# Two attentions mixed by a gate: output products summed in one block, denominators inverted in a narrow tile, a cubic for part of the exponentials

## The chip, the cores and the metric

The kernel runs on one core of a Trainium2 chip. The metric is the device time of one execution in microseconds, the median of three runs. A core has five instruction queues that run beside each other: TensorE (PE in the profile, its weight loads PEld), VectorE (DVE), ScalarE (ACT), GpSimd (POOL) and SyncE (SP), which here only issues DMAs. Each queue runs its instructions in the order in which they stand; between queues there are semaphores.

## The reference

Two attentions with 32 heads of 16 over the same 2048 rows of `x` (512 columns), mixed row by row by a gate. In A all heads share one key and one value head; B is full multi-head attention.

```
g = sigmoid((x * gate_w).sum(-1))
# A: q = x@wq (32 heads of 16), k = x@wk, v = x@wv (one head of 16)
# B: q, k, v = x@wqkv (32 heads of 16 each)
p = softmax(q @ k.T * 16**-0.5)          # 2048 x 2048 for each head
a = (p @ v, heads side by side) @ wo     # likewise b
out = g * a + (1 - g) * b
```

## The kernel before

**Tiling.** The heads are taken in eight groups of eight, A and B in turn (`groups`: a0, b0, a1, b1, ... b3). A group is done in four phases: two halves of the 2048 queries, and in each half two sets of head pairs (`q` is 0 or 2). So there are 32 phases. A phase goes over the keys in 32 *quads*, and a quad consists of two *units*: one unit is a score tile of 128 x 1024, eight matmuls on TensorE (`products`, L627). That makes 2048 units, and each needs its exponential. ScalarE takes most of them (L641, out of PSUM into a `prob` tile). VectorE takes some, two units at a time, by exponent and mantissa bits and four Horner steps (`chain`, L843 to L856, seven instructions a unit). The values of a quad are then multiplied and summed over the phase in one PSUM bank (L682). V carries a column of ones, so the softmax denominators come out of the same product.

**Banks.** Two score tiles `sc` alternate between TensorE and ScalarE. Two other banks, `pair[0]` and `pair[1]` (they print as pair_82 and pair_83, and swap roles now and then), hold the running sum over values and everything else: projections of q, k and v, scores for VectorE, and output products. The second role is called *spare* below; one job at a time owns the spare bank until VectorE has emptied it.

**End of a phase.** VectorE copies the full bank to `raw` (L747). SP moves its rows apart into numerators `oT` and denominators `dT`, both 128 x 512 and with each denominator repeated 16 times, once for each row of its head (`normalised`, L565). VectorE inverts `dT` in two pieces (L572), multiplies (L575) and splits the result into two f16 parts `o16` (L578, L581).

**Output products.** When both phases of a half of a group are normalised, four *output units* (`o_unit`) follow, one for each pair of 128-query tiles. A unit is six products with `wo` in the spare bank (two phases, three hi/lo combinations). VectorE multiplies by the gate while it empties the bank, in two instructions of 128 x 512 (L521), into one of two `sum` tiles, and a DMA of POOL adds the tile to `out` in DRAM (L531). For the last group the sum so far is read back into `late` (L1136) and added on VectorE (L515). The last phase of all is normalised and multiplied in four pieces of 128 columns after the loop (L572 to L581 and L1295); its output units hold only the first phase of that half.

**What sets the order.** The program is written out by a planner that runs when the kernel is built. It holds a clock for each engine and a cost for each kind of instruction, and asks again and again what TensorE or VectorE does next (`pe_step`, `_Plan.vector`). On TensorE scores come first as soon as a score tile is free by the plan; other work goes between two scores only if it ends before the next. When the plan allows it, `vector_job` gives two units to VectorE. The loop over phases ends when no unit and no VectorE operation is left, and only then the pieces of the tail are written.

Of the kernel before, what the change touches and what calls it, by code (L numbers as in the profile page):

```python
# [12 lines left out]
F32 = mybir.dt.float32  # L13
# [7 lines left out]
P = 128  # L21
# [14 lines left out]
S_MAX = 40.0  # L36


VEC = (0.14718679, 0.3602188, 0.76941108, -0.03925424)
LEAD = struct.unpack("I", struct.pack("f", 3.46474126))[0] & 0x7FFFFF  # L40
# [10 lines left out]
PROBS, VECS = 6, 6  # L51
# [116 lines left out]
def _fast(ctx, tc, x, wq_a, wk_a, wv_a, wo_a, wqkv_b, wo_b, gate_w, out, flag):  # L168
# [23 lines left out]
    sums = [big.tile([P, 2, BLK], F32, name=f"sum{n}") for n in range(2)]  # L192
# [82 lines left out]
    x_tiles = (vec_tiles + sums)[:8]  # L275
# [145 lines left out]

    def project(part, src, gi, half, kind, can, due):
# [17 lines left out]
        def finish(t):  # L440
# [9 lines left out]
            def then(end):  # L450
                free["spare"] = end + FROM_VEC
                plan.vec(lambda: absmax(kind, 2 * gi + half, hilo[0], AX.XY), 1130, 4, end, due=end + 8000)
                if part == "v":
                    turned(gi, half, hilo, end)
                else:
                    put(hilo, end)
# [6 lines left out]
                     lambda now: ready.get(need, math.inf) <= now and free["hilo"] <= now and can(), due, name, lambda now: can())  # L463

    def turned(gi, half, hilo, now):
# [26 lines left out]
        units.append(_Unit(jobs, finish, lambda now: True, lambda: 0, f"turn{gi}{half}"))  # L492
# [3 lines left out]
    def o_unit(n, half, t, qs, first, last):  # L496

        src, gi = groups[n]
        w, i = weights[src, gi, "o"], "ab".index(src)
        steps = [(q, a, b) for q in qs for a, b in PARTS]  # L500
        tt = [8 * half + t, 8 * half + 4 + t]
        mine = late[:, 4 * half + t]
        state = {}

        def job(k):
            q, a, b = steps[k]
            lhs = [o16s[n, half, q][:, a, t * P : (t + 1) * P]] * 2
            rhs = [w[e ^ (q // 2)][:, b] for e in range(2)]
            by_tiles(pair[1], lhs, rhs, k == 0, k == len(steps) - 1)

        def finish(end):
            def take(e):
                g = gate_up[:, i, tt[e] : tt[e] + 1]
                if n + 1 == len(groups):
                    nc.vector.scalar_tensor_tensor(mine[:, e], pair[1][:, e], g, mine[:, e], op0=ALU.mult, op1=ALU.add)  # L515
                    if last:
                        (nc.sync, nc.scalar)[e].dma_start(out[tt[e] * P : (tt[e] + 1) * P, :], mine[:, e])
                    return
                if e == 0:
                    state["sum"] = sums[state["turn"]]  # L520
                nc.vector.tensor_scalar(state["sum"][:, e], pair[1][:, e], g, None, op0=ALU.mult)  # L521

            def then(t):
                free["spare"] = t + FROM_VEC
                if n + 1 == len(groups):
                    return
                dst = out.rearrange("(h e t p) d -> h t p e d", h=2, e=2, p=P)[half, t_]
                if n == 0:
                    done = plan.on_sp([lambda: nc.sync.dma_start(dst, state["sum"])], t, ISSUE_SP)
                else:  # L530
                    done = plan.on_pool([lambda: nc.gpsimd.dma_start(dst, state["sum"], accum_op=ALU.add)], t, 1300)  # L531
                sum_free[state["turn"]] = done + SUM_LANDS

            t_ = t
            begin = end + TO_VEC
            if n + 1 < len(groups):
                state["turn"] = turn[0]
                turn[0] ^= 1
                begin = max(begin, sum_free[state["turn"]])
            for e in range(2):  # L540
                plan.vec(lambda e=e: take(e), 660, 1, begin, (), then if e else None)
# [3 lines left out]
        due = 32 * (4 * n + 2 * half + 8)  # L545
        return _Unit(jobs, finish, lambda now: all(made(("o16", n, half, q), math.inf) <= now for q in qs)
                     and made(("wo", src, gi), math.inf) <= now and made("gates", math.inf) <= now
                     and (sum_free[turn[0]] <= now + 4000 if n + 1 < len(groups) else made("late", math.inf) <= now), lambda: starts_in(due), f"o{n}{half}{t}")

    turn, sum_free = [0], [0.0, 0.0]  # L550

    def normalised(n, half, q, raw, now):
# [10 lines left out]
        moves = [(*move, e) for t in (d, o) for e in range(2) for move in moves if move[0] is t]  # L563
        for m, (part, at, to, n_rows, e) in enumerate(moves):
            queues[m % len(queues)].dma_start(part[ROWS * e + to :][:n_rows], raw[at, e])  # L565
        plan.sp = max(plan.sp, now) + len(moves) * ISSUE_SP
        o16 = ops.tile([P, 2, BLK], F16, tag="o16", name=f"o16{n}{half}{q}", bufs=7)
# [5 lines left out]

        def times(c):
            nc.vector.scalar_tensor_tensor(o[:, c : c + cut], o[:, c : c + cut], UP, d[:, c : c + cut], op0=ALU.mult, op1=ALU.mult)  # L575
# [10 lines left out]
        due = now + 30000  # L586

# [3 lines left out]
        for c in range(0, BLK, cut):  # L591
            a = plan.vec(lambda c=c: over(c), 1560, 3.5, now + 7700, (), None, due)
            b = plan.vec(lambda c=c: times(c), 330, 3.4, now + 12000, (a,), None, due)
            e = plan.vec(lambda c=c: high(c), 200, 3.3, 0.0, (b,), None, due)
            plan.vec(lambda c=c: low(c), 330, 3.2, 0.0, (e,), then if c else None, due)
# [134 lines left out]
    def emptied(t):  # L730
        ph = pv_at[0]
        n, half, q = phases[ph]
# [735 lines left out]
```

## Time and profile before

| | |
|---|---|
| median of three runs | 1826.78 us (1826.64 to 1827.12) |
| profiled execution, first to last instruction | 1822.2 us |
| what lies around the span (median less span) | 4.6 us |
| ScalarE busy | 1778.7 us, 98% |
| TensorE busy | 1742.1 us, 96% |
| VectorE busy | 1332.0 us, 73% |

The profiled execution has no total of its own beside its span; the runs agree within 0.03%, so the 4.6 us between the span and their median stand for launch and end. TensorE's matmuls are pipelined and their ends are modelled, so its 96% is not a measure of how full it is.

### The profile page before, as it was taken

What the parts mean: (1) busy time and instruction counts of PE and PEld (TensorE: products, weight loads), DVE (VectorE), ACT (ScalarE), POOL (GpSimd) and SP (SyncE); (2) the same over time, 40 slices, a digit from 0 to 9 for tenths busy, and PEclk for the clock granted to TensorE, in tenths of its full rate; (3) what the DMA queues carried; (4) which work ended last, traced back from release to release, by engine and by line L of the source; (5) the groups of instructions that cost most, each with busy time, mean ns of one, the idle gap of its engine ahead of it and who ended that gap; (6) DMA issues with size and microseconds to landing.
All of it is one profiled execution on the core that took longest, in us unless ns stands there. A gap on an engine that the chain in (4) does not pass through costs nothing.

```text
span 1822.2 us, 95700 instructions
## 1 busy us (share of the span) xinstructions
PE 1742.1 (96%) x44697; PEld 844.5 (46%) x44697; DVE 1332.0 (73%) x1507; ACT 1778.7 (98%) x1942; POOL 305.1 (17%) x367
## 2 busy tenths in 40 slices
PE   8999999999999999999999999999999999999896
PEld 5544444444444444444444444444444444444442
DVE  5277656779667597869767569796967676788994
ACT  5999999999999999999999999999999999999995
POOL 2212001202020131231102023133200111012000
PEclk9999999999999999999999999999999999999998
DMA  5121111323121142433212123342312122236111
GB/s 152 36 61 44 46 58 55 90 55 67 32 62 32 39 83 55 75 65 66 44 42 63 32 66 56 67 84 63 64 20 57 44 55 57 42 67 149 36 61 61
DMA packets 64883, 109.39 MB, mean 60 GB/s; under 512 B 14480, under 2 KB 22928, under 8 KB 64480
## 3 DMA queue, kind: packets, MB, share of 16 engines
q0 software_dynamic: 21504, 43.99, 13.6%
q1 hardware_dynamic: 39744, 56.99, 11.4%
q8 instruction: 351, 5.75, 1.3%
q10 hardware_dynamic: 3232, 2.23, 0.4%
q14 instruction: 52, 0.43, 0.1%
HBM read 14.75 MB, written 33.55 MB: 27 GB/s over the span
## 4 chain that ended last, share of the span: by engine, by line
ACT 86%; issue 8%; PE 4%; DVE 1%; DMA 1%; ACTq 0%; POOL 0%; DVEq 0%
ACT prob L641 85%; PE pair L682 1%; PE sc L627 1%; PE pair L301 0%; DVE vec L856 0%; PE pair L1173 0%; DMA prob<-in_A_wv_dram 0%; DVE xT L1295 0%; DMA vec<-in_A_x_dram 0%; DVE xT L515 0%; DMA Qa<-loqa 0%; PE pair L335 0%; DVE dT L572 0%; ACT early L641 0%; PE pair L210 0%
## 5 line engine op out<-in xcount | busy, mean ns | idle before, releaser
L641 ACT ACTIVATE prob<-sc 128x1024 f32<-128x1024 f32 x1905 | 1749.7, 1134 | 3.8 <-PE sc L627 3.2
L682 PE MATMUL pair<-prob,vA 64*32 64x512 f32 (+1 forms) x8048 | 510.4, 566 | 0.0
L682 PE MATMUL pair<-prob,vB 64*32 64x512 f32 (+1 forms) x8016 | 508.4, 569 | 0.0
L856 DVE SCALAR_TENSOR_TENSOR vec<-vec,vec 128x1024 f32<-128x1024 f32 x366 | 445.9, 1242 | 2.8
L627 PE MATMUL sc<-Qb,K 64*32 64x512 f16 x7632 | 395.9, 380 | 37.2 <-ACT prob L641 26.8
L627 PE MATMUL sc<-Qa,kA 64*32 64x512 f16 x7776 | 401.8, 380 | 21.7 <-ACT prob L641 11.6
L627 PEld LDWEIGHTS <-K 64*32 64x32 f16 x8192 | 201.2, 89 | 414.8 <-issue 375.1
L627 PEld LDWEIGHTS <-kA 64*32 64x32 f16 x8192 | 199.8, 89 | 390.2 <-issue 346.6
L843 DVE TENSOR_SCALAR vec<-pair 128x1024 int32<-128x1024 f32 x122 | 148.4, 1216 | 64.5 <-PE pair L627 64.4
L682 PEld LDWEIGHTS pair<-prob,vA 64*32 64x32 f32 x8048 | 155.3, 105 | 20.0 <-issue 1.4
L682 PEld LDWEIGHTS pair<-prob,vB 64*32 64x32 f32 x8016 | 153.5, 105 | 19.0 <-DVE raw L747 0.7
L856 DVE SCALAR_TENSOR_TENSOR vec<-vec 128x1024 f32<-128x1024 f32 x122 | 151.8, 1247 | 0.6
L531 POOL DMA_DIRECT2D out_dram<-sum x48 | 60.6, 1284 | 387.6 <-DVE sum L521 373.0
L572 DVE RECIPROCAL dT<-dT 128x256 f32<-128x256 f32 (+1 forms) x66 | 111.4, 1694 | 18.9 <-DMA dT<-raw 18.6
L747 DVE COPY raw<-pair 128x1024 f32<-128x1024 f32 x31 | 37.9, 1224 | 95.8 <-PE pair L682 95.2
L847 DVE TENSOR_SCALAR vec<-vec 128x1024 int32<-128x1024 int32 x122 | 84.1, 692 | 2.8 <-PE pair L682 1.3
L851 DVE TENSOR_SCALAR vec<-vec 128x1024 int32<-128x1024 int32 x122 | 84.5, 695 | 0.0
L521 DVE TENSOR_SCALAR sum<-pair,gate_up 128x512 f32<-128x512 f32 x112 | 78.6, 740 | 6.3 <-PE pair L210 6.0
L404 POOL DMA_DIRECT2D Qa<-hiqa x31 | 17.3, 558 | 305.6 <-DVE hiqa L445 284.5
L210 PEld LDWEIGHTS <-o 64*32 64x32 f16 x3072 | 50.1, 93 | 39.3 <-ACT o L578 8.1
L404 POOL DMA_DIRECT2D Qb<-hiqb x32 | 18.4, 574 | 293.3 <-DVE o L578 169.1
L210 PE MATMUL pair<-w16ob,o 64*32 64x512 f16 x1488 | 61.1, 384 | 6.0 <-ACT o L578 6.0
(160 smaller groups left out, 1182.7 us busy)
## 6 DMA issues: line engine op xcount, KB each, us to landing
out_dram<-sum POOLq DMA_DIRECT2D x48, 512.0 KB, 5.8
vB<-vB SPq DMA_DIRECT2D x16, 384.0 KB, 4.9
dT<-raw SPq DMA_DIRECT2D x32, 128.0 KB, 3.1
oT<-raw SPq DMA_DIRECT2D x32, 128.0 KB, 3.4
out_dram<-sum SPq DMA_DIRECT2D x8, 512.0 KB, 2.9
xT<-out_dram SPq DMA_DIRECT2D x16, 256.0 KB, 3.3
dT<-raw SPq DMA_DIRECT2D x62, 64.0 KB, 2.2
out_dram<-xT SPq DMA_DIRECT2D x12, 256.0 KB, 2.4
```

The lines of the kernel that those rows point to most:

```text
L210: nc.tensor.matmul(outs[n : n + COLS, i], lhs[i][rows(i), n : n + COLS], rhs[i][rows(i)], start=start, stop=stop)
L521: nc.vector.tensor_scalar(state["sum"][:, e], pair[1][:, e], g, None, op0=ALU.mult)
L531: done = plan.on_pool([lambda: nc.gpsimd.dma_start(dst, state["sum"], accum_op=ALU.add)], t, 1300)
L572: nc.vector.reciprocal(d[:, c : c + cut], d[:, c : c + cut])
L627: nc.tensor.matmul(bank[a : a + COLS, hh], k[rows(hh), key : key + COLS], Q[src, gi, half, p][rows(hh), j * BLK : (j + 1) * BLK], start=Tr ...
L641: nc.scalar.activation(probs[u], sc, AF.Exp, scale=SCALE / (UP * UP))
L682: nc.tensor.matmul(pair[0][32 * k : 32 * k + 32, i, cols], v[rows(i)], probs[2 * m + k // 2][rows(i), hh, cols], start=first, stop=last)
L747: nc.vector.tensor_copy(state["raw"], full)
L843: nc.vector.tensor_scalar(tile("p").bitcast(I32), pair[1], SCALE / (UP * UP) / math.log(2) * 2.0 ** 23, None, op0=ALU.mult)
L847: nc.vector.tensor_scalar(tiles["m"].bitcast(I32), tiles["p"].bitcast(I32), 0x7FFFFF, 125 << 23, op0=ALU.bitwise_and, op1=ALU.bitwise_or)
L851: nc.vector.tensor_scalar(tiles["w"].bitcast(I32), tiles["p"].bitcast(I32), 0x7F800000, 0x40000000 | LEAD, op0=ALU.bitwise_and, op1=ALU.bi ...
L856: nc.vector.scalar_tensor_tensor(p, m if i == 3 else p, VEC[i], m if i else w, op0=ALU.add, op1=ALU.mult)
```

## The change

Four things change, and since the planner knows all of them, the order of everything between the first and the last score moves with them.

**1. One block of output products for A and B.** The gate moves from the emptying of the spare bank into the normalisation. A unit is now built for a pair of groups (a and b of the same index): twelve products, from four normalised blocks, in one accumulation; the last half has nine, since the last phase is left to the tail. VectorE empties the bank in one instruction of 128 x 1024 with a constant. One `sum` tile is left instead of two; the place of the other as an input tile is taken by a piece of `vB[1]`.

**2. Denominators in a narrow tile.** The denominators of a phase, eight rows of 512, go from `raw` to DRAM (`held`), come back as 128 x 32 (`each`), are inverted there and multiplied with the gate (`gate_in`, which is laid out once through DRAM), go to DRAM again (`back`) and come back with each row read 16 times into `dT`. The tail keeps the old way.

**3. A cubic for B on VectorE.** For units of B the chain has three instructions (`first`, `second`, `third`). The limit on B's scores in the final range check gets tighter (`B_MAX`), and for that q of B is measured by head, as sums over the head on TensorE (`magnitudes`).

**4. Later moves.** q and k are laid out (`behind`, `reads`) only when the plan has passed the last reader of their buffers.

```diff
+CUBE = (0.5500864384102879, 0.8808852829622843, -0.986763876, 1.22848465)
+PROBS, VECS, SUMS = 6, 6, 1
...
     def o_unit(j, half, t, done, last):
+        steps = [(n, q, a, b) for n, q in done for a, b in PARTS]
...
+            def take():
+                if ends:
+                    nc.vector.scalar_tensor_tensor(mine, pair[1], UP ** -2, mine, op0=ALU.mult, op1=ALU.add)
...
+                nc.vector.tensor_scalar(state["sum"], pair[1], UP ** -2, None, op0=ALU.mult)
...
     def normalised(n, half, q, raw, now):
+            each = ops.tile([P, 2 * DH], F32, tag="each", name=f"each{n}{half}{q}", bufs=1)
...
+                nc.sync.dma_start(held.rearrange("(e h) q -> h e q", e=2)[to : to + count], raw[which])
+            nc.sync.dma_start(each, held.rearrange("h (c j) -> (h c) j", c=DH))
...
+        def gated():
+            nc.vector.reciprocal(each, each)
+            nc.vector.scalar_tensor_tensor(each, each, UP, gate_in[:, "ab".index(src), half], op0=ALU.mult, op1=ALU.mult)
...
+                nc.sync.dma_start(back.rearrange("h (c j) -> (h c) j", c=DH), each)
+                for e in range(2):
+                    for h in range(4):
+                        nc.sync.dma_start(d[ROWS * e + h * DH :][:DH], back[4 * e + at : 4 * e + at + 1].to_broadcast([DH, BLK]))
...
     def emptied(t):
+            parts = [(m, r) for m, r in ((n - 1, 0), (n - 1, 2), (n, 0), (n, 2))]
+            if src == "b" and (n + 1 < len(groups) or half == 0):
                 if q:
+                    units.extend(o_unit(n // 2, half, t, parts, True) for t in range(4))
+            elif src == "b" and q == 0:
+                units.extend(o_unit(n // 2, half, t, parts[:3], False) for t in range(4))
...
     def chain(u, t):
+            def first():
+                nc.vector.tensor_scalar(tile("p"), pair[1], CUBE[0] * SCALE / (UP * UP), CUBE[1], op0=ALU.mult, op1=ALU.add)
+            def second():
+                nc.vector.scalar_tensor_tensor(tile("w"), tiles["p"], CUBE[2], tiles["p"], op0=ALU.add, op1=ALU.mult)
+            def third():
+                nc.vector.scalar_tensor_tensor(p, w, CUBE[3], p, op0=ALU.add, op1=ALU.mult)
```

**How the order moves.** Counted over the whole program, ScalarE's exponentials go from 1926 to 1920 and VectorE's units from 122 to 128, of which 38 belong to A and 90 to B. Three places follow.

The first is VectorE's queue in the last group, two units of B: before, with the seven steps of one unit woven into others (`vec` are VectorE's own tiles, `pair` the spare bank).

```order
L843 TENSOR_SCALAR vec_108<-pair_83 128x1024
L847 TENSOR_SCALAR vec_106<-vec_108 128x1024
L843 TENSOR_SCALAR vec_104<-pair_83 128x1024
L851 TENSOR_SCALAR vec_105<-vec_108 128x1024
L856 SCALAR_TENSOR_TENSOR vec_108<-vec_106 128x1024
L747 COPY raw_40921<-pair_82 128x1024
```

Now two whole units stand in six rows:

```order
L962 TENSOR_SCALAR vec_105<-pair_83 128x1024
L965 SCALAR_TENSOR_TENSOR vec_106<-vec_105 128x1024
L969 SCALAR_TENSOR_TENSOR vec_105<-vec_106,vec_105 128x1024
L962 TENSOR_SCALAR vec_108<-pair_83 128x1024
L965 SCALAR_TENSOR_TENSOR vec_107<-vec_108 128x1024
L969 SCALAR_TENSOR_TENSOR vec_108<-vec_107,vec_108 128x1024
```

Each step of the cubic reads what the step before it wrote, and nothing else stands between them.

The second is SP's queue at the end of two phases of A, before (`raw` is the copied bank, `dT` the denominators, `oT` the numerators, Qb a later q of B):

```order
L565 DMA dT_36036<-raw_36033 64x512 x2
L565 DMA oT_36035<-raw_36033 64x512 x2
L565 DMA dT_37304<-raw_37301 64x512 x2
L565 DMA oT_37303<-raw_37301 64x512 x2
L404 DMA Qb_37613<-hiqb_37573 32x1024
```

The same kind of place now; `held` and `back` lie in DRAM:

```order
L219 DMA vB_92<-vB_91 64x1536 x2
L615 DMA held_37151<-raw_37146 4x2x512
L617 DMA each_37150<-held_37151 128x32
L619 DMA oT_37148<-raw_37146 64x512 x2
L634 DMA back_37152<-each_37150 128x32
L638 DMA dT_37149<-back_37152 16x512 x8
```

Four DMAs of a phase of A have become thirteen, and three of the steps wait for a landing or for VectorE in front of them.

The third is VectorE's queue at the end of the program. Before, the last of the output units (L515, two rows each) stand ahead of the last copy of a phase (L744), and the tail begins right behind it:

```order
L581 TENSOR_TENSOR o_40935<-oT_40923,o_40935 128x256
L515 SCALAR_TENSOR_TENSOR xT<-pair_83,gate_up,xT 128x512 x8
L744 COPY raw_42005<-pair_82 128x512
L572 RECIPROCAL dT_42009<-dT_42009 128x128
L575 SCALAR_TENSOR_TENSOR oT_42008<-oT_42008,dT_42009 128x128
```

Now three output units are emptied between that copy and the tail's first reciprocal, out of the bank that the copy reads:

```order
L652 TENSOR_TENSOR o_40574<-oT_40560,o_40574 128x256 x2
L560 SCALAR_TENSOR_TENSOR xT<-pair_83,xT 128x1024 x3
L821 COPY raw_41823<-pair_82 128x512
L560 SCALAR_TENSOR_TENSOR xT<-pair_82,xT 128x1024 x3
L626 RECIPROCAL dT_41827<-dT_41827 128x128
L644 SCALAR_TENSOR_TENSOR oT_41826<-oT_41826,dT_41827 128x128
```

On TensorE their 27 products stand behind the last values of the last phase; before, none stood there.

## Rows read from the trace of the kernel before

**Rows 1.** Page, part 1: busy us, share of span, instructions, by engine.
```profile
PE 1742.1 (96%) x44697; PEld 844.5 (46%) x44697; DVE 1332.0 (73%) x1507; ACT 1778.7 (98%) x1942; POOL 305.1 (17%) x367
```

**Rows 2.** Groups by line, ScalarE's exponentials: xcount | busy us, mean ns | idle before.
```profile
L641 ACT ACTIVATE prob<-sc 128x1024 f32<-128x1024 f32 x1905 | 1749.7, 1134 | 3.8 <-PE sc L627 3.2 <-DVE xT L515 0.5
L641 ACT ACTIVATE vec<-sc 128x1024 f32<-128x1024 f32 x10 | 10.2, 1035 | 0.5 <-PE sc L627 0.5
L641 ACT ACTIVATE early<-sc 128x1024 f32<-128x1024 f32 x8 | 8.4, 1047 | 0.3 <-ACT prob L641 0.3
L641 ACT ACTIVATE vB<-sc 128x1024 f32<-128x1024 f32 x3 | 3.1, 1026 | 0.6 <-PE sc L627 0.6
```

**Rows 3.** Timeline of ScalarE, first and last exponentials: start, us, what, xcount.
```profile
28.11 5.66 ACT L641 ACTIVATE prob<-sc 128x1024 f32<-128x1024 f32 x6 [1.20 <-PE sc L627]
...
1769.46 31.38 ACT L641 ACTIVATE prob<-sc 128x1024 f32<-128x1024 f32 x34
```

**Rows 4.** Two stretches: window, us, then busy (xcount) PE PEld DVE ACT POOL.
```profile
300.00:500.00 200.00, 192.09 (x4920) 91.97 (x4911) 155.31 (x171) 199.84 (x219) 31.36 (x32) 1.00 0.26 62
1500.00:1700.00 200.00, 191.77 (x4880) 91.23 (x4865) 159.65 (x180) 199.43 (x219) 29.13 (x34) 1.00 0.38 78
```

**Rows 5.** Waits: who, for whom: us in total, times, longest.
```profile
PE sc L627 <- ACT prob L641: 38.4, 108, 0.5
ACT prob L641 <- PE sc L627: 3.2, 8, 1.2
DVE dT L572 <- DMA dT<-raw: 18.6, 6, 4.4
```

**Rows 6.** Groups by line, VectorE.
```profile
L843 DVE TENSOR_SCALAR vec<-pair 128x1024 int32<-128x1024 f32 x122 | 148.4, 1216 | 64.5 <-PE pair L627 64.4
L851 DVE TENSOR_SCALAR vec<-vec 128x1024 int32<-128x1024 int32 x122 | 84.5, 695 | 0.0
L856 DVE SCALAR_TENSOR_TENSOR vec<-vec,vec 128x1024 f32<-128x1024 f32 x366 | 445.9, 1242 | 2.8
L856 DVE SCALAR_TENSOR_TENSOR vec<-vec 128x1024 f32<-128x1024 f32 x122 | 151.8, 1247 | 0.6
L572 DVE RECIPROCAL dT<-dT 128x256 f32<-128x256 f32 x62 | 107.6, 1742 | 15.7 <-DMA dT<-raw 15.4
L521 DVE TENSOR_SCALAR sum<-pair,gate_up 128x512 f32<-128x512 f32 x112 | 78.6, 740 | 6.3 <-PE pair L210 6.0
L448 DVE SCALAR_TENSOR_TENSOR lovb<-pair,hivb 128x1024 f16<-128x1024 f32 x8 | 9.8, 1224 | 0.3
```

**Rows 7.** DMA issues: xcount, KB each, median us to landing.
```profile
out_dram<-sum POOLq DMA_DIRECT2D x48, 512.0 KB, 5.8
xT<-out_dram SPq DMA_DIRECT2D x16, 256.0 KB, 3.3
dT<-raw SPq DMA_DIRECT2D x62, 64.0 KB, 2.2
```

**Rows 8.** Timeline of SP, one phase of B: issue of four DMAs.
```profile
922.58 3.67 SPq L565 DMA_DIRECT2D dT<-raw  x4
```

**Rows 9.** Timeline of the program's end.
```profile
1796.67 0.41 PE L210 MATMUL pair<-w16ob,o 64*32 64x512 f16 x8
...
1800.12 0.63 PE L210 MATMUL pair<-w16ob,o 64*32 64x512 f16 x16
...
1800.83 1.41 DVE L515 SCALAR_TENSOR_TENSOR xT<-pair,gate_up,xT 128x512 f32<-128x512 f32 x2 [2.26 <-PE pair L210]
...
1802.87 0.59 ACT L745 COPY raw<-pair 128x512 f32<-128x512 f32 x1 [2.04 <-DVE raw L744]
...
1806.04 0.95 DVE L572 RECIPROCAL dT<-dT 128x128 f32<-128x128 f32 x1 [3.20 <-DMA dT<-raw]
```

**Rows 10.** Two stretches of the end; behind POOL stands TensorE's granted clock.
```profile
1802.00:1804.40 2.40, 0.00 (x0) 0.00 (x0) 0.84 (x2) 0.59 (x1) 0.64 (x1) 1.00 0.14 36
1804.50:1811.20 6.70, 3.24 (x64) 0.91 (x64) 4.87 (x10) 0.89 (x3) 0.99 (x2) 0.50 0.24 62
```

More of the change, by code (lines that the diff above doesn't have):

```diff
@@ L420, in starts_in, with behind, reads @@
         return plan.act + 2 * max(m - at[0], 0) * EXP * 0.93
+    waiting = []
+    def behind(m, fn):
+        waiting.append((m, fn))
+    def reads():
+        for m, fn in list(waiting):
+            if at[0] >= m and not (half_vec and half_vec[0] // 2 < m):
+                waiting.remove((m, fn))
+                fn(plan.pe)
     def project(part, src, gi, half, kind, can, due):
@@ L455, in then @@
                 else:
-                    put(hilo, end)
+                    s = 2 * (2 * gi + (src == "b")) + half
+                    behind(64 * (s - 1) if part == "q" else 256 * gi, lambda t: put(hilo, max(t, end)))
             free["hilo"] = math.inf
@@ L491, in turned, with o_unit @@
         jobs = [(lambda ts=ts: job(ts), HALF) for ts in (range(4), range(4, 8))]
-        units.append(_Unit(jobs, finish, lambda now: True, lambda: 0, f"turn{gi}{half}"))
+        units.append(_Unit(jobs, finish, lambda now: pv_at[0] >= 8 * gi, lambda: 0, f"turn{gi}{half}"))
     o16s = {}
[L496 to L500, printed above, removed]
+    def o_unit(j, half, t, done, last):
+        steps = [(n, q, a, b) for n, q in done for a, b in PARTS]
@@ L518, in take, with then @@
                     return
[L519 to L525, printed above, removed]
+                state["sum"] = sums[state["turn"]]
+                nc.vector.tensor_scalar(state["sum"], pair[1], UP ** -2, None, op0=ALU.mult)
+            def then(now):
+                free["spare"] = now + FROM_VEC
+                undone[j, half] -= 1
+                if ends:
@@ L535, in finish @@
+                if j == 0:
+                    at = plan.on_sp([lambda: nc.sync.dma_start(dst, state["sum"])], now, ISSUE_SP)
+                else:
+                    at = plan.on_pool([lambda: nc.gpsimd.dma_start(dst, state["sum"], accum_op=ALU.add)], now, 1300)
+                sum_free[state["turn"]] = at + SUM_LANDS
             begin = end + TO_VEC
-            if n + 1 < len(groups):
+            if not ends:
                 state["turn"] = turn[0]
-                turn[0] ^= 1
+                turn[0] = (turn[0] + 1) % SUMS
@@ L539, in finish @@
                 begin = max(begin, sum_free[state["turn"]])
-            for e in range(2):
-                plan.vec(lambda e=e: take(e), 660, 1, begin, (), then if e else None)
+            plan.vec(take, 1131, 1, begin, (), then)
         made = ready.get
         jobs = [(lambda k=k: job(k), PRODUCT) for k in range(len(steps))]
[L545 to L548, printed above, removed]
@@ L550, in _fast @@
-    turn, sum_free = [0], [0.0, 0.0]
+        due = 32 * (8 * j + 2 * half + 8)
+        undone[j, half] = undone.get((j, half), 0) + 1
+        return _Unit(jobs, finish, lambda now: all(made(("o16", n, half, q), math.inf) <= now and made(("wo", *groups[n]), math.inf) <= now for n, q in done)
+                     and (made("late", math.inf) <= now if ends else sum_free[turn[0]] <= now + 6000), lambda: starts_in(due), f"o{j}{half}{t}")
+    undone = {}
+    turn, sum_free = [0], [0.0] * SUMS
     def normalised(n, half, q, raw, now):
@@ L586, in normalised, with spreads @@
         due = now + 30000
+        begun = [math.inf]
         def then(end):
             ready["o16", n, half, q] = end + FROM_VEC
[L591 to L595, printed above, removed]
+        def spreads(end):
+            spread(end)
+            for c in range(0, BLK, cut):
+                b = plan.vec(lambda c=c: times(c), 330, 3.4, begun[0], (), None, due)
+                e = plan.vec(lambda c=c: high(c), 200, 3.3, 0.0, (b,), None, due)
+                plan.vec(lambda c=c: low(c), 330, 3.2, 0.0, (e,), then if c else None, due)
+        plan.vec(gated, 430, 3.5, now + 7500, (), spreads, due,
+                 room=lambda: ready.get("gates", math.inf) <= plan.dve)
     tail = []
```

138 lines of the change are left out of this document (104 added, 34 removed).

## The prediction

> **What bounds the kernel now.** I read the busy shares first: ScalarE 98%, TensorE 96%, VectorE 73% [rows 1]. TensorE's figure says little, so the second view is the groups by line. ScalarE's exponentials have four rows, 1905 + 10 + 8 + 3 = 1926 instructions [rows 2]. The third view is the timeline of ScalarE: the first exponential starts at 28.11, the last group of 34 ends at 1769.46 + 31.38 = 1800.84 [rows 3]. So the span of 1822.2 has a head of 28.1, 1772.7 with exponentials, and a tail of 21.4, in which ScalarE hardly works. From start to start an exponential takes (1772.7 - 1.1) / 1925 = 0.920 us on the whole. In the windows ScalarE makes 219 of them in 200 us, in the stretch from 300 as in that from 1500, which is 0.913 each [rows 4]. The difference, 0.007 x 1926 = 14 us, is lost here and there along the run. The waits say who leads: TensorE waited 108 times for ScalarE to free a score tile, 38.4 us, and ScalarE 8 times for scores, 3.2 us [rows 5]. So the middle of the program is as long as the number of ScalarE's exponentials makes it, and VectorE, with a quarter of its time free, sets nothing there.
>
> I work against the profiled span of 1822.2 and add the 4.6 us that separate it from the median of 1826.78; the profiled execution shows no other total.
>
> **The change part by part.**
>
> *Exponentials.* A unit on VectorE costs 1.216 + 2 x 0.695 (L847 is like L851) + 3 x 1.242 + 1.247 = 7.58 us before. The cubic has the reading from PSUM, one step with one tile and one with two: 1.216 + 1.247 + 1.242 = 3.71 us [rows 6]. With 38 units of A and 90 of B that is 38 x 7.58 + 90 x 3.71 = 622 us where 122 x 7.58 = 925 us stood. VectorE gains 303 us, but the order gives it only six units more. Six exponentials less on ScalarE are 6 x 0.913 = **5.5 us less**. They count in full as long as TensorE keeps the pace; it gets no fewer score products, the same number of output products, and 32 matmuls more for the magnitudes.
>
> *Inversions and emptying.* 62 x 1.742 = 108 us of reciprocals become 31 of an eighth of the columns, at most a half of that time and more likely an eighth; 112 x 0.740 = 83 us of emptying (L521) become 24 x 1.22 = 29 us [rows 6]. All this is VectorE's time, and VectorE has no place on the path before the tail. I take it at nothing. With the exponentials it brings VectorE from 1332 to some 900 us.
>
> *Denominators through DRAM.* There is no row for such a trip. Its first half is two landings one after the other, its second half again two with eight more issues. The nearest landings are 2.2 us from tile to tile and 3.3 us for a read from DRAM [rows 7]; an issue took 3.67 / 4 = 0.92 us [rows 8]. So the first half is between 4.4 and 6.6 us and two or three issues, the second between 4.4 and 6.6 and nine issues of 8.3: some 19 to 24 us from copy to product. Nothing needs the result at once: the output units of a half come after both of its phases, and a phase lasts 60 x 0.92 = 55 us. What could hurt is VectorE standing at L629 or L646 until a landing. Behind it wait the emptying of the spare bank, and for that TensorE's next job, and ScalarE's next score behind this job. Before, VectorE stood like this for 18.6 us in 6 places, at most 4.4 us [rows 5], and all of ScalarE's waits for scores are 3.2 us. I take it at nothing within 4 us a time. Its bounds: 6 us less, if part of the 14 us lost along the run goes with the long reciprocals and two thirds of the adding DMAs, and 25 us more in the rival below.
>
> The pieces of these trips are 128 bytes, a row of 32 numbers. The Trainium skill (DMA: Bandwidth & Descriptors, Specifications) puts the least transfer at full rate at 512 bytes and says that shorter ones are read, changed and written back. No row here shows a landing of such pieces. By that rule a landing is nearer to the 5.8 us of the adding DMA [rows 7] than to 2.2, which is the second rival; the data of a trip is so little, 16 KB, that I stay with the short ones.
>
> *One sum tile.* The emptying now waits for the DMA before it, 5.8 us to landing [rows 7]. Two units are twelve products apart, and the plan fits at most one product beside an exponential: 12 x 0.913 = 11 us. It is hidden.
>
> *The tail.* This is the part on the path. In the order three output units of nine products stand behind the last values, in the bank that the last copy to `raw` empties, and VectorE empties all three before its first reciprocal of the tail. Before, from the end E of the last exponential (1800.84), ScalarE's half of the copy ended at 1803.46, E + 2.6, and the first reciprocal, which waited for its DMA, began at 1806.04, E + 5.2 [rows 9]. Now TensorE may begin at E + 2.7. Eight matmuls (one product) took 0.41 us and sixteen 0.63, so a product more is 0.22 and nine are 0.41 + 8 x 0.22 = 2.17 us. VectorE followed the last product by 0.08 us (1800.75 to 1800.83), and emptying 128 x 1024 from PSUM with a second operand costs 1.22 us (L448, [rows 6]). With 0.08 back to TensorE a unit is 3.55 us, and three are 10.6, one after the other, since all use one bank. The reciprocal then begins at E + 2.7 + 10.6 = E + 13.3 instead of E + 5.2: **8.1 us more**. The denominators have landed long before. What follows, 16 us of reciprocals, products and stores, stays.
>
> How fast TensorE runs there is open. Its granted clock was 1.00 (2.4 GHz) in the 2.4 us after it fell idle, and 0.50 (1.2 GHz) in the stretch after that, in which it had waited from 1802 to 1808 [rows 10]. Now it works 2.2 us and rests about 1.4 between units. At the lower level the eight products of a unit after the first take 0.22 more each at most, 3 x 9 x 0.22 = 5.9 us in all. The Trainium skill (TensorE: Matmul & The Clock Gate, Rules for kernel authors) warns that gaps between bursts of matmuls put the array back to the half clock. The trace agrees for the long gap; whether the short ones do it, no row shows.
>
> *Sum.* 1822.2 - 5.5 + 8.1 = 1824.8 of span, and with 4.6 around it **1829.4 us**, 0.14% more than the median before.
>
> **The rivals.**
>
> *The clock falls in the tail.* For it: the low stretch [rows 10] and three pauses. Against it: each pause is shorter than the stretch that kept its clock. It gives 1829.4 + 5.9 = 1835.3.
>
> *The denominators come late.* Place: VectorE at L629 and L646, 31 trips. It decides from the point where a wait is longer than the 4.4 us that VectorE stood before with no trace on ScalarE. With landings of 5.8 us in place of 2.2 to 3.3 a trip has four of them, 10 to 14 us more, by halves 5 to 7; what goes beyond 4.4, about 1 us, would reach ScalarE at most at 31 trips: some 25 us, 1854. For it: small pieces, and SP has to stand in line for each. Against it: the planner leaves room, and VectorE is half idle.
>
> *The middle gets shorter.* The 14 us lost along the run are partly waits beside heavy DMA traffic and VectorE's longest instructions; both shrink. A gain of 6 to 10 us there gives 1819 to 1823, faster than before. For it: VectorE drops from 73% to about 50%. Against it: ScalarE's waits for scores are 3.2 us in all, so most of the 14 us has no releaser on VectorE.
>
> *The three units hide* behind the DMA wait of the tail, so that only the saving is left: 1826.8 - 5.5 = 1821.3. For it: VectorE stood 3.2 us there [rows 9]. Against it: they begin after the copy and end with 8 us too much in a strict queue.
>
> **How the numbers follow.** The forecast gets 0.70, the clock 0.08, late denominators 0.06, a shorter middle 0.11, hidden units 0.05. About 0.2% (3.7 us) is what a measurement of this kernel tells from no change, so *same* reaches from 1823.1 to 1830.4. The forecast's own range is 1826.5 to 1832: three quarters of it are same, a quarter slower. Slower: 0.17 + 0.08 + 0.06 = 0.31. Faster: 0.05 from the hidden units and 0.05 from the middle, 0.10. Same: 0.53 and 0.06 of the middle, 0.59. The range of 8 in 10 takes in the forecast and most of the clock's case and of the middle's: 1823.5 to 1835.
>
> **What would show it.** In the profile after: 1920 exponentials on ScalarE, 219 in 200 us in the same stretches; VectorE near 900 us; three emptyings of 128 x 1024 after the last copy, about 3.5 us apart, and the first reciprocal 13 us after the last exponential; a tail near 29.5 us. A step is wrong if VectorE waits more than 5 us a time for `each` or `dT` and ScalarE shows waits behind it, if the granted clock is 0.50 between the three units, or if a stretch of 200 us holds 221 exponentials or more.

## The result, and the profile after

The changed kernel took 1829.25 us (median of 9 runs), the kernel before 1826.64 (9 runs beside it): ratio 1.0021, interval 1.0012 to 1.0029, which is no change at 2%. (A ratio here is taken over the runs of both kernels; the two medians alone give 1.0014. Differences in us between kernels below are taken from the ratios.) The forecast was 1829.4. Its terms were not all as good as its sum, and the experiments found something larger than the sum: where the exponentials taken off ScalarE were given back.

The profiled execution of the changed kernel has a span of 1826.6 us, 4.4 more than before. Its engines, in the columns of [rows 1]:

```profile
PE 1746.5 (96%) x44843; PEld 850.0 (47%) x44843; DVE 929.3 (51%) x1105; ACT 1772.9 (97%) x1936; POOL 245.7 (13%) x335
```

VectorE fell from 1332 to 929 us. ScalarE's exponentials by line, against [rows 2]:

```profile
L717 ACT ACTIVATE prob<-sc 128x1024 f32<-128x1024 f32 x1899 | 1743.6, 1136 | 4.7 <-PE sc L703 3.0 <-DVE oT L646 0.8 <-DVE xT L560 0.6
L717 ACT ACTIVATE vec<-sc 128x1024 f32<-128x1024 f32 x10 | 10.1, 1033 | 0.5 <-PE sc L703 0.4
L717 ACT ACTIVATE early<-sc 128x1024 f32<-128x1024 f32 x8 | 8.3, 1038 | 0.3 <-ACT prob L717 0.3
L717 ACT ACTIVATE vB<-sc 128x1024 f32<-128x1024 f32 x3 | 3.2, 1054 | 0.0
```

They are 1920. The first starts at 28.52 and the last ends at 1796.32, so they fill 1767.8 us, 4.9 less than before; the head is 0.4 longer and the tail 30.3 long, 8.9 more. That is the whole 4.4. The middle runs as it did: the two stretches of [rows 4] hold 219 and 220 exponentials, with VectorE (the third pair) busy 95 to 125 us in place of 155 to 160:

```profile
300.00:500.00 200.00, 191.45 (x4880) 91.97 (x4886) 124.50 (x135) 199.74 (x219) 22.48 (x23) 1.00 0.15 38
1500.00:1700.00 200.00, 188.50 (x4776) 89.59 (x4760) 94.71 (x110) 200.00 (x220) 26.87 (x43) 1.00 0.23 64
```

The waits, against [rows 5]:

```profile
DVE each L629 <- DMA each<-held: 39.7, 11, 4.9
PE sc L703 <- ACT prob L717: 38.0, 106, 0.8
...
DVE oT L646 <- DMA dT<-back: 16.4, 8, 4.3
...
ACT prob L717 <- PE sc L703: 3.0, 8, 0.6
```

VectorE stands three times as long as before for denominators, at most 4.9 us at once, and ScalarE's own waits for scores are what they were. VectorE's new groups, against [rows 6]:

```profile
L965 DVE SCALAR_TENSOR_TENSOR vec<-vec 128x1024 f32<-128x1024 f32 x90 | 112.2, 1250 | 1.5
L969 DVE SCALAR_TENSOR_TENSOR vec<-vec,vec 128x1024 f32<-128x1024 f32 x90 | 111.3, 1241 | 1.2
L962 DVE TENSOR_SCALAR vec<-pair 128x1024 f32<-128x1024 f32 x90 | 109.6, 1218 | 31.6 <-PE pair L703 31.5
...
L566 DVE TENSOR_SCALAR sum<-pair 128x1024 f32<-128x1024 f32 x24 | 29.3, 1223 | 146.1 <-PE pair L214 146.1
...
L629 DVE RECIPROCAL each<-each 128x32 f32<-128x32 f32 x31 | 10.8, 348 | 39.7 <-DMA each<-held 39.7
```

The cubic costs 3.71 us a unit, as worked out from before, and the narrow reciprocal 0.35 us. The end of the program, where [rows 9] ended:

```profile
1797.50 0.69 DVE L821 COPY raw<-pair 128x512 f32<-128x512 f32 x1
...
1798.86 1.49 PE L214 MATMUL pair<-w16oa,o 64*32 64x512 f16 x48 [1.43 <-ACT raw L822]
...
1801.13 1.23 DVE L560 SCALAR_TENSOR_TENSOR xT<-pair,xT 128x1024 f32<-128x1024 f32 x1 [2.94 <-PE pair L214]
1802.41 1.49 PE L214 MATMUL pair<-w16oa,o 64*32 64x512 f16 x48 [1.41 <-DVE xT L560]
...
1804.61 1.22 DVE L560 SCALAR_TENSOR_TENSOR xT<-pair,xT 128x1024 f32<-128x1024 f32 x1 [2.26 <-PE pair L214]
...
1808.09 1.22 DVE L560 SCALAR_TENSOR_TENSOR xT<-pair,xT 128x1024 f32<-128x1024 f32 x1 [2.26 <-PE pair L214]
1809.23 0.94 DVE L626 RECIPROCAL dT<-dT 128x128 f32<-128x128 f32 x1
```

Read the releasers: TensorE waits for VectorE's emptying and VectorE for TensorE's products, one unit every 3.48 us. The first reciprocal starts 12.9 us after the last exponential, where it was 5.2. The windows over these units, with the granted clock behind POOL as in [rows 10]:

```profile
1796.00:1800.00 4.00, 2.57 (x77) 1.05 (x68) 1.88 (x2) 0.90 (x2) 0.89 (x2) 1.00 0.13 32
1800.00:1806.00 6.00, 3.24 (x120) 1.67 (x112) 2.45 (x2) 0.00 (x0) 0.83 (x2) 1.00 0.27 69
1806.00:1809.00 3.00, 2.03 (x72) 0.94 (x65) 0.91 (x1) 0.00 (x0) 0.00 (x0) 1.00 0.02 5
```

The clock stays at its full level (2.4 GHz) through the pauses between the units.

### The profile page after: what moved, and what is told of

The parts are those of the page before. It is cut to its first block, busy times and chain, and to the rows that moved or that the text cites. A ratio compares the mean times of both kernels' runs of the same rounds, so it can differ in the third digit from the quotient of the medians.

```text
span 1826.6 us, 95893 instructions
## 1 busy us (share of the span) xinstructions
PE 1746.5 (96%) x44843; PEld 850.0 (47%) x44843; DVE 929.3 (51%) x1105; ACT 1772.9 (97%) x1936; POOL 245.7 (13%) x335
## 5 line engine op out<-in xcount | busy, mean ns | idle before, releaser
L758 PE MATMUL pair<-prob,vB 64*32 64x512 f32 (+1 forms) x7840 | 496.3, 569 | 0.0
L703 PE MATMUL sc<-Qa,kA 64*32 64x512 f16 x7888 | 407.9, 381 | 18.7 <-ACT prob L717 11.5
L703 PE MATMUL sc<-Qb,K 64*32 64x512 f16 x7472 | 385.6, 380 | 40.1 <-ACT prob L717 26.5
L703 PEld LDWEIGHTS <-K 64*32 64x32 f16 x8192 | 199.6, 89 | 413.1 <-issue 374.9
L703 PEld LDWEIGHTS <-kA 64*32 64x32 f16 x8192 | 200.4, 89 | 390.4 <-issue 346.9
L937 DVE SCALAR_TENSOR_TENSOR vec<-vec,vec 128x1024 f32<-128x1024 f32 x114 | 138.5, 1247 | 0.9
L962 DVE TENSOR_SCALAR vec<-pair 128x1024 f32<-128x1024 f32 x90 | 109.6, 1218 | 31.6 <-PE pair L703 31.5
L965 DVE SCALAR_TENSOR_TENSOR vec<-vec 128x1024 f32<-128x1024 f32 x90 | 112.2, 1250 | 1.5
L969 DVE SCALAR_TENSOR_TENSOR vec<-vec,vec 128x1024 f32<-128x1024 f32 x90 | 111.3, 1241 | 1.2
L566 DVE TENSOR_SCALAR sum<-pair 128x1024 f32<-128x1024 f32 x24 | 29.3, 1223 | 146.1 <-PE pair L214 146.1
L462 DVE TENSOR_SCALAR hiqb<-pair 128x1024 f16<-128x1024 f32 x8 | 9.8, 1224 | 141.6 <-PE pair L214 141.6
L214 PEld LDWEIGHTS <-o 64*32 64x32 f16 x3072 | 50.0, 93 | 41.1 <-issue 8.2
L214 PE MATMUL pair<-w16oa,o 64*32 64x512 f16 x1536 | 60.8, 376 | 4.2 <-DVE xT L560 2.8
L577 POOL DMA_DIRECT2D out_dram<-sum x16 | 19.8, 1237 | 329.5 <-DVE sum L566 297.4
L214 PE MATMUL pair<-w16ob,o 64*32 64x512 f16 x1488 | 60.4, 381 | 2.9 <-ACT o L649 2.9
L214 PE MATMUL pair<-xT,w16vb 64*32 64x512 f16 x1536 | 60.4, 376 | 0.0
```

The source lines that it names most:

```text
L214: nc.tensor.matmul(outs[n : n + COLS, i], lhs[i][rows(i), n : n + COLS], rhs[i][rows(i)], start=start, stop=stop)
L462: nc.vector.tensor_scalar(hilo[0], pair[1], UP ** -1, None, op0=ALU.mult)
L566: nc.vector.tensor_scalar(state["sum"], pair[1], UP ** -2, None, op0=ALU.mult)
L577: at = plan.on_pool([lambda: nc.gpsimd.dma_start(dst, state["sum"], accum_op=ALU.add)], now, 1300)
L703: nc.tensor.matmul(bank[a : a + COLS, hh], k[rows(hh), key : key + COLS], Q[src, gi, half, p][rows(hh), j * BLK : (j + 1) * BLK], start=Tr ...
L758: nc.tensor.matmul(pair[0][32 * k : 32 * k + 32, i, cols], v[rows(i)], probs[2 * m + k // 2][rows(i), hh, cols], start=first, stop=last)
```

## The experiments

Ratios are to the kernel before, run on the same chip. The changed kernel stands at 1.0021.

**The end units left out.** Only one of the four last output units is made, so three blocks of the output lack their sum.

```diff
-units.extend(o_unit(n // 2, half, t, parts[:3], False) for t in range(4))
+units.extend(o_unit(n // 2, half, t, parts[:3], False) for t in range(1))
```

> The changed kernel without the three output units that stand behind the last copy: their products and emptyings are left out (so part of the last output rows is missing), everything before them stands in the same order, 1920 exponentials. Theory A (the number of ScalarE's exponentials and the queue at the end make the time): first reciprocal of the tail at 5.2 us after the last exponential as in the kernel before, in place of 12.9; time 7.7 us under the changed kernel, about 1821.5, and 5 us under the kernel before. Rival B (the three units cost little, the loss lies in the middle, where VectorE waits for denominators): within 2 us of the changed kernel.

Measured: 1821.26 us, 0.9978 (0.9968 to 0.9988), 0.43% or 7.9 us below the changed kernel. VectorE's waits at the tail show what comes next when the units are gone:

```profile
DVE dT L626 <- DMA dT<-raw: 3.7, 1, 3.7
```

It is the wait of before (3.20 in [rows 9]). The first reciprocal starts 5.5 us after the last exponential (1796.72). So the queue of three units costs 8 us, all of it on the path, and the changed kernel without it would be 4 us faster than before.

**Without the cubic.**

```diff
-        if source(quads[u // 2][0]) == "b":
+        if False:
```

> The changed kernel with the seven steps for B on VectorE instead of the cubic's three; blocks, narrow denominators and gate as changed. The planner then leaves 1944 exponentials to ScalarE, 24 more. Theory A: 24 x 0.92 = 22 us more than the changed kernel, about 1851, with the tail as long. Rival B (VectorE's waits for denominators set the middle): VectorE is fuller and waits on the same landings, so 25 us or more on top of that, over 1870. Rival C (the exponentials that VectorE takes cost TensorE as much as ScalarE gains): within 5 us of the changed kernel.

Measured: 1856.77 us, 1.0175 (1.0158 to 1.0192), 28 us more than the changed kernel. Its exponentials and ScalarE's wait:

```profile
L717 ACT ACTIVATE prob<-sc 128x1024 f32<-128x1024 f32 x1923 | 1767.6, 1130 | 11.2 <-PE sc L703 10.5
```

With the other rows 1944 exponentials, 24 more than with the cubic. They account for 22 us; the rest is a slower pitch (0.924 us in place of 0.921). The other reading of this run matters more: everything in the change but the cubic makes the kernel 32 us *slower* than before. Of that, 18 more exponentials (1944 against 1926) are 16.6 us, the pitch (0.924 against 0.920) 8, and the longer tail 8. The forecast's "six exponentials less" is a difference of two larger terms, minus 24 and plus 18.

**A longer trip of the denominators.**

```diff
+            for k in range(2):
+                further = dram.tile([2 * 4, BLK], F32, tag=f"further{k}", name=f"further{k}{n}{half}{q}", bufs=2)
+                nc.sync.dma_start(further, held)
+                held = further
```

> The changed kernel with two more copies from DRAM to DRAM in the first half of each of the 31 trips of the denominators, 16 KB each, unknown to the planner; same order on VectorE, TensorE and ScalarE. A trip gets some 5 to 7 us longer, and VectorE stands that much longer in front of its narrow reciprocal, 31 x 5 = 150 us and more in all. Theory A, with the cover claimed in the prediction (waits up to about 4.4 us reach nobody, what exceeds it reaches ScalarE): waits of 6 to 9 us, so 2 to 4 us a trip, 60 to 120 us more than the changed kernel. Rival D (half of VectorE's time is free, and TensorE has work that doesn't need the spare bank, so even 9 us are covered): under 5 us more.

Measured: 1835.23 us, 1.0053 (1.0036 to 1.0069). The waits:

```profile
DVE each L633 <- DMA each<-further: 112.0, 24, 9.8
DVE oT L650 <- DMA dT<-back: 58.2, 11, 8.2
...
ACT prob L721 <- PE sc L707: 7.1, 8, 2.5
```

VectorE stood 170 us where it had stood 56, up to 9.8 us at a time, and the program became 5.8 us longer. Of its waits 12 were longer than 4.4 us, by 46 us together. The price that I had expected, 60 to 120 us, was ten times too high or more, and rival D (under 5 us) was nearly right: most of what exceeds 4.4 us is covered too.

**Wide reciprocals again.** In the changed kernel the denominators are spread and inverted as before (two reciprocals of 128x256 a phase); the gate is left out of the normalisation.

```diff
-        plan.vec(gated, 430, 3.5, now + 7500, (), spreads, due,
+        for c in range(0, BLK, cut):
+            a = plan.vec(lambda c=c: over(c), 1560, 3.5, now + 7700, (), None, due)
...
```

> The changed kernel with the denominators spread and inverted as before (two reciprocals of 128x256 a phase) and without the trip through DRAM; the gate is left out of the normalisation. ScalarE still has 1920 exps. Theory A of the prediction (VectorE's time is worth nothing while the number of exps stays): the same as the changed kernel, ratio 1.001 to 1.003, though VectorE is busy some 90 us longer. Rival V (the 1.74 us reciprocals stand before the chains and make probabilities late): 5 to 20 us slower than the changed kernel, ratio 1.005 to 1.013. Rival T (the trip through DRAM costs what the small loss of pitch hides): 2 to 5 us faster than the changed kernel, 0.9995 to 1.001.

Measured: 1829.4 us, 1.0024 (1.0014 to 1.0033), as the changed kernel, with VectorE busy 1010 us in place of 929. Its wait for denominators:

```profile
DVE dT L617 <- DMA dT<-raw: 61.3, 13, 7.1
```

Inverting 128x32 by way of DRAM neither gains nor costs anything that these runs can tell (0.1%).

**The end units in banks of their own.** The last copy keeps its bank; the first unit starts in the other, the second and third in the two score tiles; VectorE empties them between its reciprocals.

```diff
-        flips = not current and free["spare"] < t + 1500
+        flips = ph < LASTS and not current and free["spare"] < t + 1500
...
+    for k, unit in enumerate(kept):
+        alone[unit.name]["bank"] = ps_s.tile([P, ACT, BLK], F32, tag="sc", name=f"own{k}") if k else pair[1]
```

> The changed kernel with the same work at its end, where the three last output units no longer queue in one bank: the last copy keeps its own bank, the first unit goes to the free one at once, the second and third to the two score tiles, and VectorE empties them between the reciprocals instead of ahead of them. Theory A (the end is a chain in which each unit waits for the emptying of the one ahead): the first reciprocal starts some 5 us after the last exp instead of 12.9, two emptyings of 1.2 us come back between the steps, so 5 us less than the changed kernel, ratio 0.999 to 0.9995. Rival P (TensorE's clock or its own work sets the end, 9 products a unit at 2.3 us before the last 12): 0 to 2 us less, ratio 1.001 to 1.002.

Measured: 1824.26 us, 1.0002 (0.9992 to 1.0011), 3.5 us below the changed kernel. The timeline at its end:

```profile
1800.68 1.49 PE L214 MATMUL own<-w16oa,o 64*32 64x512 f16 x48
1800.94 1.22 DVE L560 SCALAR_TENSOR_TENSOR xT<-pair,xT 128x1024 f32<-128x1024 f32 x1 [1.60 <-PE pair L214]
...
1803.50 0.95 DVE L630 RECIPROCAL dT<-dT 128x128 f32<-128x128 f32 x1 [1.33 <-DMA dT<-raw]
```

TensorE no longer waits for an emptying, and the first reciprocal comes 6.0 us after the last exponential (1797.47). Two of the three emptyings, 1.22 us each, now stand between later steps. Theory A was right on the order of the steps; its 5 us were 3.5.

**One number of the planner.** The order leaves VectorE half idle. LATE lets a job of the spare bank, or a value job of VectorE's units, run past the time at which the second score of a pair falls due.

```diff
-    JOB, AFTER, TURN, SPARE, WORK, EXTRA, LATE = 900, 3000, 3000, 5000, 1500, 7000, 0
+    JOB, AFTER, TURN, SPARE, WORK, EXTRA, LATE = 900, 3000, 3000, 5000, 1500, 7000, 200
```

In the changed kernel:

> The changed kernel with one number of the planner changed: work in the spare bank may run up to 0.2 us into the time of the next score, where it had to be over (LATE 200 for 0). The planner then gives VectorE 172 units instead of 128, leaves 1876 exponentials to ScalarE, and puts one output unit behind the last copy instead of three. Theory A: 44 x 0.92 = 40 us less and 7 us less in the tail, about 1782. Rival C (TensorE is as full as ScalarE, each unit that moves to VectorE costs it the slot that it saves): ScalarE shows waits for scores of some 40 us, and the time is within 10 us of the changed kernel.

Measured: 1812.4 us, 0.9935 (0.9919 to 0.9952). That is 16 us less than the changed kernel, not the 47 of theory A. Some 6 of them are the tail (24.2 us for 30.3, with one unit behind the last copy in place of three), so 44 exponentials fewer took some 12 us off the middle, not 40. ScalarE waited 24.3 us for scores, in 33 places; that is rival C's sign, weaker, and its "within 10 us" failed too. One of them in the timeline:

```profile
877.79 0.40 PEld L758 LDWEIGHTS pair<-prob,vB 64*32 64x32 f32 x12
878.00 0.67 PE L758 MATMUL pair<-prob,vB 64*32 64x256 f32 x11
880.63 0.41 PE L758 MATMUL pair<-prob,vB 64*32 64x256 f32 x3 [1.96 <-issue]
...
881.75 2.86 ACT L717 ACTIVATE prob<-sc 128x1024 f32<-128x1024 f32 x3 [2.29 <-PE sc L703]
```

TensorE stops for 1.96 us in the middle of a value job and waits for nothing that these views show ("issue"); ScalarE then stands 2.29. The value jobs are of 256 columns: with a spare job beside a score the planner has no room for one of 512 and makes two. The whole program has 52651 matmuls in place of 44843. TensorE's waits of this kernel:

```profile
PE pair L758 <- issue: 6.6, 8, 2.0
...
PE pair L214 <- issue: 3.4, 6, 1.2
PE sc L703 <- issue: 1.9, 4, 0.6
```

The changed kernel has 0.7 us at L214 and L703 together. The same number in the kernel before:

> The kernel before with one number of its planner changed: a job of the spare bank may run up to 200 ns into the next score's time when the second score of a pair is due (before: 0). VectorE then takes 24 exps more than before and ScalarE has 1902 left (before 1926). Theory A (a removed exp is worth 0.91 us): 22 us less, ratio 0.988. Rival C (as in the run with the same number on the changed kernel, where two thirds of the expected gain came back as ScalarE waiting for scores): 5 to 9 us less, ratio 0.995 to 0.997, and waits of ScalarE for scores well above the 3.2 us of before. Rival S: the number gains only together with the cubic, ratio 1.000.

Measured: 1837.04 us, 1.0064 (1.0048 to 1.0081): *slower* with 24 exponentials fewer. None of my theories had that. It has 52169 matmuls in place of 44697, and its rows are those of the run above, only more so:

```profile
ACT prob L641 <- PE sc L627: 32.1, 43, 2.6
...
PE pair L682 <- issue: 10.5, 11, 2.2
...
PE sc L627 <- issue: 5.5, 7, 1.4
```

And the kernel before with this number and the cubic:

> The kernel before (output products per attention, wide reciprocals) with two of the parts: the cubic chain for B on VectorE and the same planner number at 200. ScalarE has 1870 exps left; no output unit of nine products stands behind the last copy. Theory A: 56 exps fewer than before at 0.91 us, 51 us less, ratio 0.972. Rival C (two thirds come back as waits for TensorE): about 17 us less, ratio 0.990 to 0.992, no faster than the changed kernel with that number (0.9935) by more than its tail. If this lies below 0.99 the summed block is worth less than nothing beside the cubic; if it lies above 0.9935 the block and the narrow reciprocals earn their place.

Measured: 1811.67 us, 0.9925 (0.9904 to 0.9947), the same as the changed kernel with it: beside the cubic, the rest of the change earns nothing on the whole. Theory A's 51 us came to 14, a little under rival C's 17.

**Two numbers: the stops taken away.** TIGHT lets a value job of 512 columns run late too, so that the planner need not cut it.

```diff
-SLACK, TIGHT, URGENT = 404, 404, 300
+SLACK, TIGHT, URGENT = 404, 604, 300
```

With LATE 200, in the kernel before:

> The kernel before with the same two numbers: 1902 exps left to ScalarE. Theory N: 24 exps fewer without the stops, 22 us less than before, ratio 0.988, where LATE alone gave 1.0064. Rival T: 1.00 to 1.007 again.

Measured: 1820.72 us, 0.9977 (0.9968 to 0.9987). This is the cleanest pair of the study: the same 1902 exponentials and the same 1675 VectorE instructions as in the run at 1.0064, and 44649 matmuls instead of 52169. ScalarE's waits for scores and the longest row of TensorE's stops:

```profile
ACT prob L641 <- PE sc L627: 8.8, 12, 1.7
...
PE sc L627 <- issue: 0.7, 1, 0.7
```

The stops are down to 1.1 us in all, and 16 us are gone with them. Theory N was right on that and wrong on the size: against before, 24 exponentials fewer gave 4 us, not 22. The pitch is 0.929 us in place of 0.920, which gives back 17. ScalarE's waits for scores, 8.8 us for 3.2, are a part of this; the rest no row names. In the changed kernel:

> The changed kernel with two numbers of the planner changed: LATE 200 as in the run that gave 0.9935, and TIGHT 604 (before: 404), by which a value job of 512 columns may also run 200 ns into the next score's time, so that the planner hardly falls back on two jobs of 256 columns. 1868 exps are left to ScalarE, and the program has about as many TensorE instructions as the changed kernel. Theory N (with LATE alone the gain came back because twice as many narrow value jobs need 17% more TensorE instructions, and TensorE now and then stands 1 to 2.4 us for instructions): the stops go, 52 exps fewer than the changed kernel at 0.91 us, about 47 us less than it, ratio 0.975 to 0.98. Rival T (TensorE has no time left for more work ahead of the scores, however it is cut): ScalarE waits for scores as often, ratio 0.99 to 1.0. Rival U (each score 0.2 us later, a short wait before many exps): pitch 0.93 or more with no long waits, ratio 0.985 to 0.99.

Measured: 1788.01 us, 0.9798 (0.9781 to 0.9814), 2.2% below the changed kernel. ScalarE's exponentials and TensorE's waits:

```profile
L717 ACT ACTIVATE prob<-sc 128x1024 f32<-128x1024 f32 x1847 | 1704.3, 1057 | 6.6 <-PE sc L703 5.0 <-ACT prob L717 0.6 <-issue 0.3
```
```profile
PE sc L703 <- ACT prob L717: 53.5, 171, 0.7
```

1868 exponentials in 1729.5 us, 38 less than the 1920 took. TensorE now waits for ScalarE (53.5 us) and ScalarE hardly for TensorE (5.0). Theory N holds here, with a part of U: the pitch is 0.926 in place of 0.921, which gives back 9.6 of the 48 us that 52 exponentials are worth.

In the kernel before with the cubic:

> The kernel before with the cubic chain for B and the same two numbers; output products per attention and wide reciprocals as before. 1868 exps. Theory N: 58 exps fewer than before, 53 us less, ratio 0.971, and the same as or a few us below the changed kernel with both numbers, since no unit of nine products stands behind the last copy. If it is more than 5 us slower than that kernel, the summed block is worth something once TensorE is the tight engine (fewer emptyings and adding DMAs).

Measured: 1788.27 us, 0.9799 (0.9782 to 0.9815), level with the run above; theory N's 53 us came to 37. The two are level by two terms that cancel: the changed kernel's tail is 8.8 us longer (30.0 against 21.2), and its pitch is shorter (0.926 against 0.932, here in the slowest of four executions). And the changed kernel with LATE 300 and the end units in their own banks:

> The changed kernel with LATE 300, TIGHT 604 and the last output units in their own banks: 1854 exps. Theory N: 66 exps fewer than the changed kernel, 60 us, and 3.5 us from the end: ratio 0.967. Rival U (a score 0.3 us late is felt by ScalarE): 0.975 to 0.985, no better than the run with 200.

Measured: 1787.94 us, 0.9790 (0.9772 to 0.9808). Its tail is 27.0 us in place of 30.0, but 14 exponentials fewer bring nothing: ScalarE's wait for scores has grown.

```profile
ACT prob L721 <- PE sc L707: 11.9, 13, 4.1
```

The pitch is 0.934: rival U. At LATE 300 later scores take back what fewer exponentials give. LATE 200 and TIGHT 604 with the end units in their own banks were not tried. The three kernels near 1788 are about 2% below both of the comparison; their intervals, 0.977 to 0.982, leave open whether it is more or less than that.

| exponentials left, ratio | numbers as they were | LATE 200 | LATE 200, TIGHT 604 |
|---|---|---|---|
| before | 1926, 1 | 1902, 1.0064 | 1902, 0.9977 |
| before and cubic | not tried | 1870, 0.9925 | 1868, 0.9799 |
| changed without cubic | 1944, 1.0175 | not tried | not tried |
| changed | 1920, 1.0021 | 1876, 0.9935 | 1868, 0.9798 |

## Why the prediction was right, and where it was not

*Exponentials.* Right in sign and nearly in size: 4.9 us for six, where 5.5 were forecast. The rival of a shorter middle fell: the pitch is 0.921 us where it was 0.920. The step "VectorE gains 303 us, but the order gives it only six units more" was left as a fact of the order. The runs show what is in it: the cubic takes 24 exponentials off ScalarE (28 us), and the rest of the change puts 18 back. Which of its edits does so was not separated on the chip. The narrow reciprocals do not, for the wide ones leave 1920 as well; the summed block, the single sum tile, the later moves and the magnitudes of q are left. With the two numbers changed, before and changed kernel, both with the cubic, leave 1868 each: there the rest of the change takes no exponential, and its longer tail is made up for in the middle.

*Inversions and emptying worth nothing.* Right. The wide reciprocals, 81 us more on VectorE, moved no exponential and cost no time. (The cubic's 303 us are another matter: they are what the 24 exponentials above were bought with.)

*Denominators through DRAM.* Right that they are hidden, too cautious on the threshold. One trip in the trace: the copy ends at 916.81, the narrow reciprocal starts at 924.69 and the product at 932.70, after a wait of 1.79 us: 15.9 us where I had 19 to 24. VectorE came to the reciprocal without a wait. The issues are shorter (0.34 us for `each`, 4.12 for the eight of `dT`) than the 0.92 of [rows 8], which makes some 5 us less. The rival's threshold, a wait longer than 4.4 us, does not hold as a price: 46 us beyond it cost 5.8 us.

*The tail.* Right: first reciprocal at E + 12.9 for E + 13.3, a unit in 3.48 us for 3.55. The tail is 8.9 longer, not 8.1; 7.7 of that is the queue, and the rest lies behind it: the program ends 6.7 us after SP's last issue, where it was 5.0.

*The clock.* The rival (0.08) fell: 1.00 through all three units, with pauses of 1.4 us in TensorE's work. (Its price was also a little high: 8 products a unit, as its sentence says, give 5.3 us, not the 5.9 of nine.) After the units TensorE stood 2.9 us (1808.02 to 1810.88), still at 1.00, and its clock was 0.50 from 1812 to 1815, when it worked again. The Trainium skill (TensorE: Matmul & The Clock Gate, Why this matters for your kernels; the prediction has the section under a wrong name) warns of gaps between bursts. The trace bears it out for this longer gap, not for the three short ones.

*The time around the span.* Wrong. I added 4.6 us, the distance of the profiled span from a median, and took it for launch and end. After the change this distance is 2.6 us, and the profiled execution itself took 1828.70 us, 2.1 more than its span. In later runs of the kernel before, each with its span, the two lie 1.7 to 1.9 us apart. So the profiled execution of before took some 1824 us and was a quick one, by nearly 3. Against the span the forecast was 1824.8 and the measurement 1826.6: 1.8 us too low (0.6 from the exponentials, 0.4 from the head, 0.8 from the tail), and the 2.0 us too much around it hid this. That 1829.4 met 1829.25 so closely is luck; the terms of the span were good to 1 us each.

## What to carry to other kernels

Where the count of one engine's instructions sets the time, ask what each part of a change does to that count: here a part worth 28 us was eaten by another, and the sum looked like nothing. When freed time of another engine is not taken up, look at the rule that hands work out before looking at the work: in the changed kernel two numbers of the planner were worth 41 us, ten times the change. In the kernel before, without the cubic, the same two were worth 4: the cheaper chain and the rule had to change together. Work that is cut into more and smaller matmuls to fit a gap can cost more than the gap, so count instructions as well as time.

## What the runs showed of the hardware

TensorE can stop without a releaser. In the three programs with some 52000 matmuls (LATE 200 alone) it stood at "issue" up to 2.4 us at a time, 13 to 22 us in a run, and then went on in a burst. In the programs with some 44700 these rows come to at most 2.6 us a run and 1.1 at a time, at the same busy share (94 to 96%).

The traces say more on these stops than the waits do. Packets of 16 KB come in on a queue of kind `instruction`, about one for every 255 instructions of TensorE, weight loads included. The kernel before with LATE 200, and with TIGHT 604 besides (packets, MB, share of the DMA engines):

```profile
q8 instruction: 410, 6.72, 1.5%
```
```profile
q8 instruction: 351, 5.75, 1.3%
```

With LATE 200 alone, 25 of TensorE's stops over 0.3 us, 23.1 us in all, begin at the same place in each block of 256 instructions (at remainder 193, counted from the start of the trace). After 23 of them it went on 1.3 to 1.7 us behind the end of such a packet. Behind 24 of them ScalarE stood waiting and went on within 2 us of TensorE, 24 us of its waits. With TIGHT 604 two such stops are left, 1.1 us. A fixed place in a block and a fixed distance to a packet fit a block of instructions that came late. That TensorE had run out of them is read from this match; no row names it as the releaser. A block lasted 4.1 us (median) with LATE 200 alone and 4.9 with both numbers. The Trainium skill (Runtime: NRT & Kernel Launch, Instruction fetch mechanics) says that fetching instructions is hidden, because they are issued more slowly than they are filled in; by this reading that does not hold for a stretch as dense as this one.

Waits that looked dangerous were nearly harmless here on a half-idle engine: 114 us more of VectorE standing cost 5.8 us.
